# Moving weight roundings, stack loads, the last maxima and three loads of attended values in a two-layer attention and spectral kernel

## The chip, the cores and the metric

The kernel runs on one core of one Trainium2 chip. The time is the device time of one execution in microseconds (us); lower is better. Several runs are given for each kernel, and one further execution was recorded by the hardware profiler, which yields the trace that the rows below come from. The engines are PE (matmul), DVE (VectorE), ACT (ScalarE), POOL (GpSimd) and SP, which here only issues DMAs.

## The reference

Two layers are applied twice in turn to x, 2048 tokens of 576 features, all in float32:

```python
def _A_ref(x, wqkv, wo):               # called on layernorm(x)
    q, k, v = ...                      # x @ wqkv, 32 heads of 18
    scores = einsum("bhqd,bhkd->bhqk", q, k) * 18 ** -0.5
    # causal, sliding window of 256: 0 <= query - key < 256
    p = softmax(where(mask, scores, -1e9))
    return (p @ v) @ wo

def _B_ref(x, w_r, w_i):               # called on layernorm(x)
    return irfft2(rfft2(x) * (w_r + 1j * w_i), s=(S, D))

for _ in range(2):
    x = x + _A_ref(layernorm(x), A_wqkv, A_wo)
    x = x + _B_ref(layernorm(x), B_w_r, B_w_i)
```

## The kernel before

**Number format.** The products are float32 by splitting: a matrix is rounded to the type fp32r and the remainder is kept beside it, so that a product is a sum of three (high by high, high by low, low by high). For a weight block of the query and key projections the rounding `wqh` is a cast on ACT (L698) and the remainder `wql` a subtraction on POOL (L699; DVE for one block); `w_split(i)` issues both, and then `w_load(i + 2)`, a DMA on SP's queue (L896), into the buffer `wqr` that both have just read. That DMA therefore waits for the remainder.

**Stages of a layer A.** First the layernorm and the value projection. Then the query and key projections: nine blocks of 128 columns (i = 0 to 8), each for four chunks of 512 tokens (c = 0 to 3), fourteen matmuls each. A result `sg` (high and low, 512 KB) is sent to DRAM (`qk_d`, the send at L1145) and loaded back in another arrangement as stacks `qs` and `ks` of one group of four heads (`stack_load`, L1162). There are eight groups, and the stacks of two groups are held at a time. A stack of one group and one chunk comes in four pieces (two for q, two for k) of three DMAs of 72 KB.

**Rounds.** A round is one group of four heads and one tile of 128 tokens, 16 rounds a group, 128 in all. For round y the kernel first takes the row maxima of the scores (S on PE at L1187, the maximum on DVE at L1189), ten rounds ahead of the round x = y - 10 whose transposed scores E (L1219) go through the exponential on ACT (L1220) into a tile P, masked by selects on POOL (L1222, L1225). The maxima of four tiles (one chunk) are collected, transposed on PE (`tpm`), copied on ACT (`mt`, L1201) and written by two DMAs of 4 KB on SP's queue into one row of `qs` (L1203, `m_rows`), so that the score matmul itself subtracts them. E of round x reads tiles x, x+1 and x+2 of its group.

**The order of the work** is written out by hand. Ten opening rounds (t = -10 to -1) take maxima and seven matmuls of projections each. Then 59 mixed blocks p = 0 to 58 take two rounds each: for rounds 2p and 2p+1 eight S for ten rounds ahead and eight E, between them the matmuls of the projections, each in two halves on the two halves of the PE array (results `pj`, `pk`). Behind them stands what is called the value block here: the halves just ended are copied by ACT (L1129) and added by POOL (L1133, `total`), what is planned for the `end` of the block runs (send, divide and others), then U = P times v for rounds 2p-2 and 2p-1 (L1240), and in odd blocks `m_rows` of chunk (2p + 9) // 4. Work planned `early` stands ahead of the block's second score step and work planned `mid` in its middle. `loads(t)` issues the stack loads and `behind(t)` the work for the output projection. Twelve tail rounds follow (t = 118 to 129), which have no projections and no maxima, and then the output projection with the following layer B.

**Shared buffers.** The first projections' results `sg` of block i = 2 stand in buffers of the tag "P", six in number, which the tiles P take next: the exponentials of rounds 2 to 5 wait until these results have been sent.

**SP's queue** issues strictly in order, some 0.36 us for each DMA, and each DMA also waits for the one eight before it.

**The output projection** (class `Out`) is prepared in late rounds: `room` and `weights` load wo, `split` rounds it (cast on ACT at L751, remainder on POOL), `const` and `filters` load tables, `load_x` the residual, `attended(z, half)` loads results of three parts of the attention (512 KB each, L774) into `oraw`. Part 3 holds the last groups: its rows come through `store` (`op_d` from `o`, L1275), `pack` (L1282) and `attended(3, ...)` (L777); the very last group goes from `o7` straight into its place (L1278).

## Time and profile before

| | us |
|---|---|
| median of 3 runs | 1313.33 |
| lowest, highest | 1306.14, 1315.49 |
| the profiled execution | 1308.3 |
| its span | 1306.6 |
| PE busy in it | 1271.4 (97%) |
| first layer: mixed blocks, from 127.5 to | 423.3 |
| first layer: tail rounds, to | 445.3 |
| second layer: mixed blocks, from 796.3 to | 1091.4 |
| second layer: tail rounds, to | 1113.0 |

The mean granted clock of PE over the execution is 0.995. The starts of the value products U mark the blocks: the products of block p are the stretch of rows of L1240 with the same start in the timeline of PE. Rows of the timeline give start, duration, engine, line, operation, output and inputs, the number of instructions, and in brackets the idle time before them and what ended it.

### The profile page before, as it was taken

The page shows a single profiled execution, that of the slowest core. Times are in us where ns is not written, and L with a number is a line of the kernel's source. Part 1 is how long each engine was busy: PE and PEld are TensorE (multiplying, and loading weights), DVE is VectorE, ACT ScalarE, POOL GpSimd, SP SyncE. Part 2 cuts the span into 40 slices and gives each one's busy share as a digit, 9 for nine tenths or more (in the row PEclk, how much of TensorE's full clock was granted, in tenths as well). Part 3 has the DMA queues.
Part 4 walks back from the last instruction along what each step waited for, and adds up shares of the span by engine and source line. Part 5 has one row for each costly group of instructions (what it writes and reads, how often), then busy time and mean ns, then how long its engine had stood idle before and what let it go on. Part 6 is the DMA issues. An engine that isn't in the chain of part 4 may idle for free.

```text
span 1306.6 us, 35490 instructions
## 1 busy us (share of the span) xinstructions
PE 1271.4 (97%) x12115; PEld 1004.0 (77%) x12115; DVE 950.9 (73%) x3192; ACT 784.7 (60%) x1944; POOL 777.0 (59%) x1252
## 2 busy tenths in 40 slices
PE   9999999999999899999999999999999999899998
PEld 8986666666678699975989976666666676897587
DVE  5417799999999577766674148989999986575755
ACT  5532788888876544533355315788878868473233
POOL 2158788998877444567221196788878776113721
PEclk9999999999999999999999999999999999999999
DMA  6847666666666647688873368666666668497874
GB/s 204 222 150 210 211 210 222 229 205 195 206 218 204 181 135 229 199 272 252 281 253 77 88 209 221 201 221 199 206 196 191 201 206 258 134 348 257 278 256 163
DMA packets 179497, 274.37 MB, mean 210 GB/s; under 512 B 67743, under 2 KB 77727, under 8 KB 177989
## 3 DMA queue, kind: packets, MB, share of 16 engines
q1 hardware_dynamic: 167007, 243.63, 59.4%
q0 software_dynamic: 4656, 13.44, 4.0%
q10 hardware_dynamic: 7654, 15.03, 3.3%
q8 instruction: 97, 1.59, 0.5%
q14 instruction: 83, 0.68, 0.2%
HBM read 164.54 MB, written 114.81 MB: 214 GB/s over the span
## 4 chain that ended last, share of the span: by engine, by line
PE 79%; DMA 8%; ACT 4%; DVE 4%; POOL 2%; issue 2%; SPq 1%; DVEq 0%; ACTq 0%; POOLq 0%
PE pj L1115 11%; PE U L1240 11%; PE vps L1005 9%; PE S L1187 8%; PE pk L1115 7%; PE ops L802 7%; PE E L1219 5%; PE po L274 4%; PE pq L524 3%; PE p L503 2%; PE pf L274 2%; ACT P L1220 2%; PE pi L600 2%; DMA op_d<-o 2%; PE pz L312 2%
## 5 line engine op out<-in xcount | busy, mean ns | idle before, releaser
L1189 DVE CUSTOM_DVE_ANT_0 jk<-S,mask 128x384 bf16<-128x384 f32 (+2 forms) x1024 | 481.3, 527 | 31.1 <-PE S L1187 11.8
L1220 ACT ACTIVATE P<-E 128x384 f32<-128x384 f32 (+2 forms) x1024 | 411.7, 479 | 86.4 <-PE E L1219 41.9
L1219 PE MATMUL E<-qs,ks 64*128 64x384 f32 (+2 forms) x1024 | 320.8, 369 | 8.2 <-ACT P L1220 4.2
L1187 PE MATMUL S<-ks,qs 63*128 63x384 f32 (+2 forms) x1024 | 324.6, 370 | 1.1 <-issue 0.5
L1222 POOL TENSOR_SCALAR_AFFINE_SELECT P<-P 128x512 f32<-128x512 f32 x256 | 163.2, 637 | 119.5 <-ACT P L1220 114.1
L1219 PEld LDWEIGHTS E<-qs,ks 64*128 64x128 f32 x1024 | 179.9, 185 | 55.4 <-ACT P L1220 28.3
L1187 PEld LDWEIGHTS S<-ks,qs 63*128 63x128 f32 x1024 | 172.6, 185 | 61.3 <-DVE m L1189 36.7
L1240 PE MATMUL U<-P,vq 128*32 128x256 f32 (+2 forms) x3840 | 185.1, 329 | 0.8 <-POOL P L1222 0.8
L1240 PEld LDWEIGHTS U<-P,vq 128*32 128x32 f32 (+1 forms) x3840 | 107.1, 109 | 75.4 <-issue 11.1
L1115 PE MATMUL pj<-xh,wqh 64*128 64x512 f32 (+1 forms) x360 | 151.9, 422 | 0.0
L1225 POOL TENSOR_SCALAR_AFFINE_SELECT P<-P 128x512 f32<-128x512 f32 x224 | 141.9, 634 | 0.0
L1115 PE MATMUL pj<-xh,wql 64*128 64x512 f32 (+1 forms) x360 | 138.0, 423 | 0.0
L1115 PE MATMUL pj<-xl,wqh 64*128 64x512 f32 (+1 forms) x288 | 120.6, 419 | 0.0
L802 PE MATMUL ops<-oroom 128*128 128x290 f32 (+1 forms) x812 | 114.0, 297 | 1.6 <-DVE ofree L848 1.2
L802 PEld LDWEIGHTS ops<-oroom 128*128 128x128 f32 x812 | 110.4, 189 | 2.3 <-ACT ofree L836 1.4
L1115 PE MATMUL pk<-xh,wqh 64*128 64x512 f32 x230 | 92.6, 403 | 0.0
L1115 PE MATMUL pk<-xh,wql 64*128 64x512 f32 x230 | 90.1, 396 | 0.0
L1246 DVE STREAM_TRANSPOSE us<-U 128x256 f32<-128x256 f32 x128 | 56.7, 443 | 45.2 <-PE U L1240 43.0
L1189 DVE DVE_READ_ACCUMULATOR2_ANT m<- 128x1 f32 x1024 | 85.0, 83 | 0.0
L1115 PE MATMUL pk<-xl,wqh 64*128 64x512 f32 x184 | 73.6, 400 | 0.0
L789 POOL TENSOR_TENSOR oroom<-oraw,oroom 64x128 fp32r<-64x128 f32 x26 | 13.9, 535 | 99.3 <-ACT oroom L787 49.4
L1115 PEld LDWEIGHTS pj<-xh,wqh 64*128 64x128 f32 (+1 forms) x360 | 67.1, 186 | 7.2 <-issue 1.5
(521 smaller groups left out, 2870.5 us busy)
## 6 DMA issues: line engine op xcount, KB each, us to landing
qk_d<-sg SPq DMA_DIRECT2D x56, 512.0 KB
qs<-qk_d SPq DMA_DIRECT2D x384, 72.0 KB
ks<-qk_d SPq DMA_DIRECT2D x348, 72.0 KB
op_d<-o SPq DMA_DIRECT2D x56, 256.0 KB
v_d<-vt SPq DMA_DIRECT2D x32, 304.0 KB
vq<-v_d SPq DMA_DIRECT2D x16, 608.0 KB
wt<-in_w SPq DMA_DIRECT2D x16, 580.0 KB
ofree<-x SPq DMA_DIRECT2D x16, 580.0 KB
```

Source lines behind the costliest of these rows:

```text
L274: T.matmul(ps[:, c, 0:NF], tail[r] if si == 4 else hl_(si), dcs[b // 2][r, b % 2], start=mi == si == 0, stop=si == 4)
L802: self.nc.tensor.matmul(self.ps[u][n][:, 0:self.n], x, self.w[p][:, (2 * wk + n) * self.n:(2 * wk + n + 1) * self.n], start=first and i == ...
L1005: T.matmul(ps[:, n, 0:288], xT(xk, c), w[:, wk, n * 288:(n + 1) * 288], start=i == 0, stop=i == len(ks) - 1)
L1115: T.matmul(ps.rearrange("r (n p) -> r n p", n=NT) if second else ps, w[r, wk], x[r], start=s == 0, stop=s == len(ks) - 1)
L1187: T.matmul(ps[:, 0:N], q[b:b + 63, pair, i * 128:i * 128 + 128], k[b:b + 63, pair, lo:hi], start=True, stop=True)
L1189: V.tensor_tensor_reduce(out=jk[:, 0:N], in0=ps[:, 0:N], in1=mask[:, 384 - N:384], scale=1.0, scalar=-3e38, op0=ALU.add, op1=ALU.max, accu ...
L1219: T.matmul(ps[:, 0:nq], k[b:b + 64, pair, j * 128:j * 128 + 128], q[b:b + 64, pair, j * 128:j * 128 + nq], start=True, stop=True)
L1220: A.activation(p[:, hl_, 0:nq], ps[:, 0:nq], AF.Exp, scale=SC)
L1222: P.affine_select(out=p[:, :, 0:128], in_=p[:, :, 0:128], pattern=[[0, 4], [1, 128]], compare_op=ALU.is_ge, fill=0.0, base=0, channel_mult ...
L1225: P.affine_select(out=p[:, :, 256:384], in_=p[:, :, 256:384], pattern=[[0, 4], [-1, 128]], compare_op=ALU.is_gt, fill=0.0, base=0, channel ...
L1240: T.matmul(U[32 * h:32 * h + v.shape[1], (q0 - e) * 128:(q1 - e) * 128], v, pt[n, j][:, h, (q0 - j) * 128:(q1 - j) * 128], start=j == max( ...
L1246: V.transpose(us[n, c][:, 8 * k:8 * k + 8].rearrange("r b (a p) -> r (b a) p", a=2), U[:, 0:256].rearrange("r (p n) -> r n p", n=NT))
```

## The change

Seven edits, none of which changes what is computed:

1. In the mixed blocks `w_split` is no longer issued in the midst of the projection's matmuls (step 7 of chunk 2) but collected and issued behind the block's last projection, ahead of what is planned for its end. This concerns five weight blocks per layer.
2. Stack loads of groups 1 to 7 are issued 18 rounds ahead, one piece a round, all on SP. Before, group 1 came partly whole at t = -4 and partly 12 rounds ahead, group 2's first chunk at t = 6 to 12, the rest 20 rounds ahead, and a part of group 1 on POOL's queue.
3. The projections end one block later (48 for 47 in `ends`).
4. The roundings of wo stand at the end of blocks 53 to 57 instead of in mid round; their weights' loads come four rounds later.
5. `store` stands half a block earlier.
6. The last `m_rows` is issued ahead of `behind(117)`.
7. `attended(0..2, 0)` come in rounds 112 to 114 and `attended(0..2, 1)` in rounds 118 to 120, where all six stood in rounds 112 to 117.

```diff
-            ended = []
+            ended, splits = [], []
...
                     if opens and s == 7 and c == 2 and 0 < i < 8:
-                        w_split(i + 1)
+                        if half is None:
+                            w_split(i + 1)
+                        else:
+                            splits.append(i + 1)
...
-                            (P if which and (n == 0 and c > 1 or n == 1 and c == 0) else nc.sync).dma_start(
+                            (P if which and n == 0 and c > 1 else nc.sync).dma_start(
...
-                if t == -4:
-                    stack_load(1, 0)
-                n, c = divmod(t + (12 if t < 16 else 20), NT)
-                if 4 <= t < 16 or 1 < n < NQ and t >= 12:
-                    stack_load(1 if t < 16 else n, t // 4 if t < 16 else c // 4, (t % 4,))
-                if t in range(6, 14, 2):
-                    stack_load(2, 0, ((t - 6) // 2,))
+                n, c = divmod(t + 2, NT)
+                if 0 <= n < NQ - 1:
+                    stack_load(n + 1, c // 4, (c % 4,))
...
-                ends = [1 + 47 * u // 22 for u in range(23)]
+                ends = [1 + 48 * u // 22 for u in range(23)]
...
+                for k in range(5):
+                    plan(end, last - 6 + k, out.split, k)
...
                     ended.clear()
+                    while splits:
+                        w_split(splits.pop())
                     run(end, p)
...
-                            plan(mid, p + 3, store, n, c)
+                            plan(early, p + 3, store, n, c)
...
+                    if p == last - 1:
+                        m_rows(*divmod((2 * last + LEAD - 1) // 4, 4))
                     behind(2 * p + 1)
-                m_rows(*divmod((2 * last + LEAD - 1) // 4, 4))
...
-                if t == OB - 22:
+                if t == OB - 18:
                     out.room()
-                if t - OB + 22 in range(0, 10, 2):
-                    out.weights((t - OB + 22) // 2)
-                if t - OB + 16 in range(0, 10, 2):
-                    out.split((t - OB + 16) // 2)
+                if t - OB + 18 in range(0, 10, 2):
+                    out.weights((t - OB + 18) // 2)
...
-                if 0 <= t - (OB - 8) < 6:
-                    out.attended(*divmod(t - (OB - 8), 2))
+                if t - OB in (-8, -7, -6):
+                    out.attended(t - OB + 8, 0)
+                if t - OB in (-2, -1, 0):
+                    out.attended(t - OB + 2, 1)
```

Here OB is 120, `last` 59 and LEAD 10. The lines of the kernel after are numbered three higher from the middle on (the send is L1148, the stack loads L1165, the maxima L1206, U L1243).

**The opening of the first layer, queue of SP.** The rows follow the load of a group's values; `wqr` is a weight load, `qs` and `ks` from `qk_d` are stack pieces, `qk_d` from `sg` a send, and `qs` from `mt` the maxima (here those of the third chunk of the first group). Before:

```order
L896 DMA wqr_1458<-in_wqk 128x640
L1162 DMA qs_1059<-qk_d 18x2x512 x6
L1145 DMA qk_d<-sg_2_1467 128x2x512
L1145 DMA qk_d<-sg_3_1530 128x2x512
L1145 DMA qk_d<-sg_0_1588 128x2x512
L1203 DMA qs_1058<-mt_2_1764 2x4x128 x2
```

and after:

```order
L896 DMA wqr_1458<-in_wqk 128x640
L1148 DMA qk_d<-sg_2_1467 128x2x512
L1165 DMA qs_1059<-qk_d 18x2x512 x3
L1148 DMA qk_d<-sg_3_1518 128x2x512
L1165 DMA qs_1059<-qk_d 18x2x512 x3
L1165 DMA ks_1061<-qk_d 18x2x512 x3
L1148 DMA qk_d<-sg_0_1582 128x2x512
L1165 DMA ks_1061<-qk_d 18x2x512 x3
L1165 DMA qs_1059<-qk_d 18x2x512 x6
L1206 DMA qs_1058<-mt_2_1770 2x4x128 x2
```

The sends have moved ahead of the stack pieces, and the maxima behind eighteen of them where there were six.

**Block 11 of the first layer.** On POOL stand the selects of P, the remainder (L1142) and the sum (L1133) of projections' results, and the remainder of a weight block, `wql`. Before:

```order
L1142 TENSOR_TENSOR sg_1_2635<-sg_1_2635 128x512
L699 TENSOR_TENSOR wql_2788<-wqr_1458,wqh_2787 128x640
L1222 AFFINE_SELECT P_6_2779<-P_6_2779 128x4x128
L1225 AFFINE_SELECT P_6_2779<-P_6_2779 128x4x128
L1222 AFFINE_SELECT P_7_2828<-P_7_2828 128x4x128
L1225 AFFINE_SELECT P_7_2828<-P_7_2828 128x4x128
L1133 TENSOR_TENSOR sg_2_2857<-sg_2_2857 128x512
```

and after:

```order
L1145 TENSOR_TENSOR sg_1_2629<-sg_1_2629 128x512
L1225 AFFINE_SELECT P_6_2774<-P_6_2774 128x4x128
L1228 AFFINE_SELECT P_6_2774<-P_6_2774 128x4x128
L1225 AFFINE_SELECT P_7_2816<-P_7_2816 128x4x128
L1228 AFFINE_SELECT P_7_2816<-P_7_2816 128x4x128
L1136 TENSOR_TENSOR sg_2_2845<-sg_2_2845 128x512
L699 TENSOR_TENSOR wql_2854<-wqr_1458,wqh_2853 128x640
```

The remainder of the weights has moved behind four selects and the sum. On SP's queue at the same place stand the weight load that waits for that remainder, the store of a finished result (`op_d` from `o`), stack pieces, a send, and the maxima of the second group's last chunk. Before:

```order
L896 DMA wqr_2791<-in_wqk 128x640
L1275 DMA op_d<-o_3_2749 128x512
L1162 DMA ks_1060<-qk_d 18x2x512 x3
L1145 DMA qk_d<-sg_1_2635 128x2x512
L1203 DMA qs_1059<-mt_3_2889 2x4x128 x2
```

and after:

```order
L1278 DMA op_d<-o_3_2743 128x512
L1165 DMA qs_1058<-qk_d 18x2x512 x3
L896 DMA wqr_2857<-in_wqk 128x640
L1148 DMA qk_d<-sg_1_2629 128x2x512
L1206 DMA qs_1059<-mt_3_2883 2x4x128 x2
```

The weight load now stands directly ahead of the send and the maxima; it is the same at block 3 and in the second layer.

**The end of the mixed blocks, queue of SP,** from the last table of constants on (`mt7_3` are the last maxima, `o6_3` the last result of the seventh group; `dc` tables, `ofree` from `in_x` the residual, `oraw` attended values, `oroom` the filters). Before:

```order
L758 DMA dc4_7928<-dcr_62 128x580
L774 DMA oraw1_7825<-o_d_85 128x4x256
L766 DMA ofree_6992<-in_x 128x576
L774 DMA oraw0_7762<-o_d_85 128x4x256
L762 DMA oroom_6991<-gcr_63 128x512
L774 DMA oraw1_7825<-o_d_85 128x4x256
L1203 DMA qs1_1059<-mt7_3_8035 2x4x128 x2
L1275 DMA op_d_86<-o6_3_8011 128x512
```

and after:

```order
L758 DMA dc4_7911<-dcr_62 128x580
L766 DMA ofree_7184<-in_x 128x576
L1206 DMA qs1_1059<-mt7_3_8014 2x4x128 x2
L762 DMA oroom_7183<-gcr_63 128x512
L1278 DMA op_d_86<-o6_3_7992 128x512
L766 DMA ofree_7184<-in_x 128x576
L774 DMA oraw1_8047<-o_d_85 128x4x256 x2
L1285 DMA o_d_85<-op_d_86 16x2304
```

The last maxima and the last store of the seventh group now precede the filters or follow them directly, and the loads of attended values into `oraw1` stand behind them.

## The prediction

> **What bounds the kernel now.** I read the engine shares first, then the windows by stage, then, inside the attention stage, the starts of the value blocks in the timeline of TensorE.
>
> ```profile
> PE 1271.4 (97%) x12115; PEld 1004.0 (77%) x12115; DVE 950.9 (73%) x3192; ACT 784.7 (60%) x1944; POOL 777.0 (59%) x1252
> 145.40:423.30 277.90, 276.73 (x3458) 195.38 (x3454) 253.50 (x1004) 223.96 (x551) 231.46 (x324) 1.00 0.66 210
> 423.30:445.30 22.00, 18.31 (x268) 10.21 (x265) 11.89 (x26) 16.93 (x45) 12.68 (x21) 1.00 0.82 248
> ```
>
> After the window and its length the columns are busy microseconds of PE, weight loads, DVE, ACT and POOL, the granted clock, the DMA share and GB/s. PE is busy 97% of the span, and 276.7 of 277.9 us in the first layer's mixed blocks. There a stall of PE costs its full length, and work of ACT or POOL costs only what it delays PE. The layer's tail is different: PE is busy 18.3 of 22.0 us, so 3.7 us could go there.
>
> **The opening.** The edit that touches PE first is the one to the stack loads. Before, the SP queue reads: weight load, six pieces of a stack, send of a projection, maxima.
>
> ```profile
> 132.02 0.35 SPq L896 DMA_DIRECT2D wqr<-in_wqk  x1
> 132.42 2.17 SPq L1162 DMA_DIRECT2D qs<-qk_d  x6
> 134.69 2.16 SPq L1145 DMA_DIRECT2D qk_d<-sg  x3
> 137.29 1.87 SPq L1203 DMA_DIRECT2D qs<-mt  x2
> 139.65 1.71 ACT L1220 ACTIVATE P<-E 128x384 f32<-128x384 f32 x4 [2.39 <-DMA qk_d<-sg]
> 140.20 0.64 PE L1219 MATMUL E<-qs,ks 64*128 64x384 f32 x1 [2.08 <-ACT P L1220]
> 135.62 0.86 PE L1240 MATMUL U<-P,vq 128*32 128x256 f32 x16
> 143.99 1.51 PE L1240 MATMUL U<-P,vq 128*32 128x256 f32 x32
> 140.20:143.30 3.10, 3.10 (x16) 3.10 (x18) 1.60 (x6) 2.13 (x6) 1.22 (x2) 0.51 0.82 259
> 807.24 3.38 ACT L1220 ACTIVATE P<-E 128x384 f32<-128x384 f32 x8 [1.37 <-DMA qk_d<-sg]
> ```
>
> The exponentials write into buffers from which projections are still being sent, so ACT waits 2.39 us for the send, PE waits 2.08 us for ACT, and then PE runs 3.1 us at 0.51 of the clock. The block from 135.62 to 143.99 takes 8.37 us, where a later one takes 5.14 (308.19 to 313.33, quoted below): 3.2 us too much. The second layer has the same wait, 1.37 us on ACT; PE loses between 0 and that, and I take 0.9, above the middle since PE lost 2.08 of ACT's 2.39 above. Now the send stands right behind the weight load, ahead of the six pieces (2.17 us of issue), so it starts about 2.2 us sooner and both stalls go: **minus 4.1 us**.
>
> What is late next in that queue: the maxima of chunk 2 of the first group. They stood behind one weight load, six pieces and three sends; now they stand behind the weight load, three sends and eighteen pieces. A piece takes 2.17/6 = 0.36 us to issue, so twelve more make 4.3 us, less what the queue spent waiting on sends (2.16 us for three); issue moves from 137.3 to about 140 to 142. The group's first scores that need them come behind the value block of 143.99, whose products take some 1.4 us; without the 3.2 us that is 142.2. A maxima transfer takes between these two:
>
> ```profile
> 1058.57 3.63 DMA qs<-mt
> 124.67 7.29 DMA qs<-mt
> ```
>
> With the lower one it lands at 143.6 to 145.6, 1.4 to 3.4 us late if the first layer had no slack, and less in the second, where the queue is ahead. I take 2 us for both layers together: **plus 2.0** (bounds 0 and 7).
>
> **The roundings of the projections' weights.** Five blocks per layer had the cast on ACT and the remainder on POOL in their middle. I compare two such blocks with the blocks eight further on, which have the same place in the pattern and no rounding, by the starts of the value products:
>
> ```profile
> 183.89 0.86 PE L1240 MATMUL U<-P,vq 128*32 128x256 f32 x16
> 189.13 1.07 PE L1240 MATMUL U<-P,vq 128*32 128x256 f32 x20
> 194.27 1.07 PE L1240 MATMUL U<-P,vq 128*32 128x256 f32 x20
> 223.66 1.07 PE L1240 MATMUL U<-P,vq 128*32 128x256 f32 x20
> 228.42 0.84 PE L1240 MATMUL U<-P,vq 128*32 128x256 f32 x14
> 268.31 1.06 PE L1240 MATMUL U<-P,vq 128*32 128x256 f32 x18
> 273.80 1.07 PE L1240 MATMUL U<-P,vq 128*32 128x256 f32 x20
> 308.19 1.07 PE L1240 MATMUL U<-P,vq 128*32 128x256 f32 x20
> 313.33 1.05 PE L1240 MATMUL U<-P,vq 128*32 128x256 f32 x17
> 387.26 1.07 PE L1240 MATMUL U<-P,vq 128*32 128x256 f32 x20
> 392.71 1.07 PE L1240 MATMUL U<-P,vq 128*32 128x256 f32 x20
> L698 ACT CAST wqh<-wqr x18: 710/721/761, 56.1 to 983.0; 128x640 fp32r<-128x640 f32 x18
> L699 POOL TENSOR_TENSOR wql<-wqr,wqh x16: 1551/1559/1574, 56.9 to 984.3; 128x640 fp32r<-128x640 f32 x16
> 190.88 0.27 ACT L1201 ACTIVATE mt<-tpm 16x128 fp32r<-16x128 f32 x1 [0.32 <-PE tpm L1199]
> ```
>
> 5.24 against 4.76 us, and 5.49 against 5.14: the cast costs 0.48 and 0.35, some 0.4 each, ten times 4.0 us. In the value block it lands just where ACT waits 0.32 us for the transposed maxima (the last row), so of its 0.72 us up to 0.4 stay and delay the next exponentials; PE has value products to do there. I take 0.15 each (bounds 0 and 0.4): **minus 2.5**.
>
> **The roundings of wo** move likewise, in five blocks per layer. 387.26 to 392.71 is 5.45 us against 5.14: 0.31 each, and I count all of it, since these issue no transfer: **minus 3.1** (bounds 0 and 3.1).
>
> **The new wait.** The remainder on POOL is what the next weight load waits for (it overwrites what both roundings read). While that was mid block, nobody stood behind it. Now the queue of SP reads at the end of blocks 3 and 11 of each layer: weight load, send, maxima.
>
> ```profile
> 180.18 0.64 ACT L1129 COPY sg<-pk 128x512 f32<-128x512 f32 x1
> 181.10 1.29 POOL L1133 TENSOR_TENSOR sg<-sg 128x512 f32<-128x512 f32 x1
> 188.57 0.36 SPq L896 DMA_DIRECT2D wqr<-in_wqk  x1
> 191.17 1.63 SPq L1203 DMA_DIRECT2D qs<-mt  x2
> ```
>
> Before, the weight load goes out at 188.57, ahead of the value block of 189.13, and the maxima 2.04 us after the block's start. After, POOL first adds the halves just copied: the copy ends 1.5 us after the start of a block (two copies of 0.65 and a gap), the sum takes 1.29, the remainder 1.56, so the weight load goes out after some 4.3 us; behind it the weight load's own 0.36 and a send of like length, then the two maxima transfers (0.8 apart as in the row of 191.17): the second at about 5.7. With 3.63 us it lands 9.3 us after the block's start. The scores that need it are those of the block after next, which begin one block (5.14) and the value products (1.07 by the row of 194.27, and a score step and a projection step ahead, some 0.35) later: 6.6. That is a stall of 2.7 us; because a weight load and a 512 KB send go out just ahead of it I take 2.8: **four times 2.8 = plus 11.2** (bounds 0, if the transfer is as quick as 1 us, and 4.5). The other three roundings per layer end in blocks whose maxima are either absent (even blocks) or of a group's first chunk, which is read three blocks later.
>
> Does such a stall also slow the clock? Beside the opening's 0.51 after an idle of 2.08 us, the starts of the two output projections bear on it: the granted clock is the third number from the end of a window's row.
>
> ```profile
> 445.37 0.40 PE L802 MATMUL ops_pj<-oroom 128*128 128x288 f32 x1 [2.15 <-DVE us L1246]
> 445.40:448.40 3.00, 3.00 (x22) 3.00 (x23) 2.80 (x7) 0.00 (x0) 0.00 (x0) 1.00 0.66 169
> 1113.00 0.56 PE L802 MATMUL ops_pj<-oroom 128*128 128x290 f32 x1 [2.16 <-DVE us L1246]
> 1113.00:1116.20 3.20, 3.20 (x13) 3.20 (x14) 3.00 (x7) 0.00 (x0) 0.00 (x0) 0.51 0.61 159
> ```
>
> So of three idles of 2.08, 2.15 and 2.16 us the first and the last were followed by 3.1 us at half speed (1.5 us lost). I take two of the four new stalls: **plus 3.0** (bounds 0 and 6). [...]
>
> **The tail.** Before, the last maxima are issued behind the filters and the loads of attended values, which now come later.
>
> ```profile
> 432.39 0.44 PE L1219 MATMUL E<-qs,ks 64*128 64x384 f32 x2 [1.06 <-DMA qs<-mt]
> 440.94 0.72 DVE L787 CAST oroom<-oraw 128x512 fp32r<-128x512 f32 x1 [1.31 <-DMA o_d<-op_d]
> 1100.02 0.44 PE L1219 MATMUL E<-qs,ks 64*128 64x384 f32 x2 [0.80 <-DMA qs<-mt]
> ```
>
> The waits of 1.06 and 0.80 us for the maxima go; the packed last group lands sooner, since three loads of 512 KB stand behind it instead of before it, and the 1.31 us in which DVE waited for it shrinks, in both layers. That is 1.9 plus up to 2.6; with the 1.5 us of half clock at 1113 likely gone it is 0.5 to 6. I take **minus 4.0**. The three loads delayed are needed only in the output projection; if they came late there, up to 1.5 us of this would be given back. Spreading the projections over one more block removes only idle-filling matmuls; I count nothing, and the half block by which a finished result is stored earlier is covered, since its pack comes two blocks later.
>
> **The sum**: -4.1 + 2.0 - 2.5 - 3.1 + 11.2 + 3.0 - 4.0 = +2.5 on the profiled execution's 1308.3 us, so 1311. That execution lies 5 us under the median of the runs shown (1313.3), inside their spread of 0.7%; a measurement of this kernel can tell about 1%, 13 us, from no change.
>
> **The rivals.**
> 1. *The maxima are not late* (0.22). If the remainder slips in ahead of the sum's wait, or these transfers of 4 KB land in 1 to 2 us, the four stalls and the clock term fall away: 1311 - 14.2 = 1297; with nothing lost at the opening either 1295. For it: before, none of these maxima, issued 2 us into the block, made PE wait, so they land in under 4.6 us, and how far under no row tells. Against it: the 3.63 and 7.29 us.
> 2. *The weight load blocks the queue for longer* (0.13, slower). The one mechanism is the wait at blocks 3 and 11: if the maxima land as the slower row does (7.29 instead of 3.63), each stall is 6.3 us instead of 2.8, and every one is long enough for half clock: +14 + 3 = 1328. It decides from about 5 us per stall. For it: the load and the send just ahead on the same engines. [...]
> 3. *Little moves* (0.13). The casts cost the same in the value block, and the maxima land in 2.5 us: -4.1 - 3.1/2 - 4.0/2 + 4 x 1.5 = -1.7, so 1306.6. It differs little in time from the forecast and is told from it in the trace.
>
> **How the numbers follow.** The forecast case has 0.52, about 1303 to 1320 by its bounds. Rival 1 ends at 1295 to 1298, rival 2 at 1324 to 1330. A range of 1296 to 1323 leaves out rival 2 and half of rival 1's lower edge, nearly 2 in 10. Against the runs shown, faster by over 1% means under 1300: rival 1 nearly whole, 0.21. Slower by over 1% means over 1326: most of rival 2, 0.10. The rest, 0.69, is no change.
>
> **What the profile after would show.** Right: the block from 135.62 falls from 8.4 to near 5 us with no wait for a send; the blocks with roundings fall to their counterparts; the value blocks of 3 and 11 are followed, one block later, by PE waiting 2 to 4 us for the maxima, with the weight load in the SP queue some 4 us into the block; the tail has no wait for maxima. Wrong: no such wait (then rival 1), the casts moved showing up as waits of PE for ACT right behind the value block (then less gain), or a loss in the output projection for the attended values.

## The result and the profile after

| | us |
|---|---|
| before, median of 4 runs | 1311.95 (1306.14 to 1315.49) |
| after, median of 4 runs | 1325.12 (1324.33 to 1327.96) |
| ratio, with its 95% interval | 1.0109 (1.0068 to 1.015) |
| profiled execution and span after | 1324.91 and 1323.0 |

The kernel became 1.1% slower; the forecast was 1311, and the time lies 2 us above the upper end of the range. Between the two profiled executions the difference is 16.6 us. By the page of after PE is busy for 1273.9 us, about as long as before (1271.4).

The list of waits of PE says what was added (engine, line, what it waited for, microseconds in all, times, the longest). First before, then after:

```profile
PE ops_pj L802 <- DVE us L1246: 4.3, 2, 2.2
PE E L1219 <- ACT P L1220: 4.2, 7, 2.1
PE E L1219 <- DMA qs<-mt: 2.4, 4, 1.1
```

```profile
PE E L1222 <- DMA qs<-mt: 14.1, 8, 2.7
PE ops_pj L802 <- DVE us L1249: 10.2, 2, 5.1
PE E L1222 <- ACT P L1223: 1.5, 8, 0.3
```

The wait for ACT behind the sends is nearly gone, as was forecast. In its place stand 14.1 us for maxima, and at the start of the two output projections 10.2 us where it was 4.3.

**The opening after.** Timeline of SP's queue and of PE, first layer; then two rows of the second layer and one of the chain of waits, and two windows (length, busy PE and the other engines, granted clock third from the end):

```profile
138.18 2.97 SPq L1165 DMA_DIRECT2D qs<-qk_d  x6
141.26 1.25 SPq L1206 DMA_DIRECT2D qs<-mt  x2
136.07 0.86 PE L1243 MATMUL U<-P,vq 128*32 128x256 f32 x16
140.71 1.51 PE L1243 MATMUL U<-P,vq 128*32 128x256 f32 x32
144.60 0.41 PE L1222 MATMUL E<-qs,ks 64*128 64x384 f32 x1 [2.13 <-DMA qs<-mt]
148.91 1.82 PE L1243 MATMUL U<-P,vq 128*32 128x256 f32 x32
818.84 0.29 PE L1190 MATMUL S<-ks,qs 63*128 63x128 f32 x1 [1.25 <-DMA ks<-qk_d]
821.57 0.41 PE L1222 MATMUL E<-qs,ks 64*128 64x384 f32 x1 [2.44 <-DMA qs<-mt]
141.26 3.20 DMA qs<-mt
144.60:147.90 3.30, 3.30 (x25) 3.13 (x27) 1.68 (x10) 2.41 (x6) 1.13 (x2) 0.74 0.80 246
821.57:825.00 3.43, 3.43 (x22) 3.29 (x24) 1.57 (x9) 2.11 (x5) 1.06 (x2) 0.57 1.01 236
```

The block that took 8.37 us takes 4.64 (136.07 to 140.71). The next one takes 8.20 instead of 5.24: the maxima are issued at 141.26, behind the stack pieces, and land 3.2 us later. In the second layer that block takes 10.01 instead of 5.24, since PE waits there for two things in turn: 1.25 us for a stack piece of the second group, whose first maxima are taken in this block, and 2.44 us for the maxima of chunk 2. Both stalls for the maxima were followed by a slower clock (0.74 and 0.57).

**The value blocks with a rounding.** The queue at the end of block 3 and what it did two blocks on, then the maxima and the stall of block 11, the two stalls of the second layer, and the time that the maxima took:

```profile
153.19 0.36 SPq L896 DMA_DIRECT2D wqr<-in_wqk  x1
154.13 1.49 SPq L1206 DMA_DIRECT2D qs<-mt  x2
158.01 0.41 PE L1222 MATMUL E<-qs,ks 64*128 64x384 f32 x1 [1.78 <-DMA qs<-mt]
196.30 1.47 SPq L1206 DMA_DIRECT2D qs<-mt  x2
199.78 0.41 PE L1222 MATMUL E<-qs,ks 64*128 64x384 f32 x1 [2.01 <-DMA qs<-mt]
835.83 0.66 PE L1222 MATMUL E<-qs,ks 64*128 64x384 f32 x1 [2.72 <-DMA qs<-mt]
878.86 0.41 PE L1222 MATMUL E<-qs,ks 64*128 64x384 f32 x1 [1.82 <-DMA qs<-mt]
154.13 3.75 DMA qs<-mt
196.30 3.34 DMA qs<-mt
```

The weight load goes out 4.28 us after the value products of 148.91 began, the maxima 5.2 us after. What follows the stalls, by windows, as above:

```profile
158.00:161.00 3.00, 2.99 (x27) 2.49 (x29) 2.26 (x9) 2.52 (x6) 0.78 (x2) 1.00 0.65 177
199.70:203.00 3.30, 3.22 (x19) 2.93 (x21) 2.17 (x9) 2.06 (x5) 1.41 (x3) 0.67 0.61 173
835.80:839.20 3.40, 3.37 (x18) 3.17 (x20) 1.57 (x5) 1.76 (x4) 0.59 (x1) 0.51 0.61 196
878.80:882.10 3.30, 3.24 (x20) 2.85 (x21) 2.34 (x9) 2.14 (x6) 1.64 (x3) 0.69 0.62 169
```

Three of the four stalls were followed by a slower clock (0.67, 0.51 and 0.69).

**The tail,** first before, then after (first layer; the last two rows are the output projections of both layers):

```profile
423.35 1.51 PE L1240 MATMUL U<-P,vq 128*32 128x256 f32 x32
432.98 0.55 SPq L1282 DMA_DIRECT2D o_d<-op_d  x1
435.61 1.22 SPq L777 DMA_DIRECT2D oraw<-o_d  x2
```

```profile
428.71 1.51 PE L1243 MATMUL U<-P,vq 128*32 128x256 f32 x32
433.32 1.33 SPq L774 DMA_DIRECT2D oraw<-o_d  x2
435.58 0.58 SPq L1285 DMA_DIRECT2D o_d<-op_d  x1
436.26 3.71 SPq L1281 DMA_DIRECT2D ofree<-o  x4
440.52 0.60 SPq L774 DMA_DIRECT2D oraw<-o_d  x1
441.91 1.22 SPq L777 DMA_DIRECT2D oraw<-o_d  x2
448.25 0.43 DVE L787 CAST oroom<-oraw 128x512 fp32r<-128x512 f32 x1 [4.52 <-DMA oraw<-o_d]
452.06 0.61 PE L802 MATMUL ops_pj<-oroom 128*128 128x288 f32 x1 [5.11 <-DVE us L1249]
1130.13 0.61 PE L802 MATMUL ops_pj<-oroom 128*128 128x290 f32 x1 [5.09 <-DVE us L1249]
```

No score waits for the last maxima any more, but from the last value block to the output projection it takes 23.35 us (428.71 to 452.06) where it took 22.02, and 23.34 in the second layer where it took 21.51. Two of the moved loads (433.32) stand just ahead of the first pack (L1285), and between it and the load of the last attended part (L777) stand the four stores of the last group and the third moved load. That load goes out 13.2 us after the last value block, where it took 12.3 before, although the pack goes out 2.8 us sooner after it; DVE's first cast of the output projection starts 19.5 us after the value block instead of 17.6. The output projections begin at a granted clock of 0.50 in both layers (452.06 to 456.50 and 1130.13 to 1135.00), where before only the second did; what stands behind the tails differs by less than 1 us a layer.

The table adds up the difference by the starts of the value products in both traces. For the roundings it takes the rest of each layer's mixed blocks; block 3 had a rounding of its own, some 0.5 us a layer, which lies in its own row.

| us, both layers | forecast | measured |
|---|---|---|
| sends ahead of the pieces (block 2) | -4.1 | -5.0 |
| maxima of chunk 2 (block 3) | +2.0 | +7.7 |
| weight load ahead of the maxima (blocks 5, 13), with the clock | +14.2 | +12.9 |
| roundings in the value blocks | -5.6 | -4.9 |
| tail to the output projection | -4.0 | +3.2 |
| blocks 23 and 25 of the first layer | 0 | +2.3 |
| the rest | 0 | +0.3 |
| sum | +2.5 | +16.4 |

### The profile page after: what moved, and what is told of

Read it like the earlier page. It is cut to its first block, busy times and chain, and to the rows that moved or that the text cites. A ratio compares the mean times of both kernels' runs of the same rounds, so it can differ in the third digit from the quotient of the medians.

```text
span 1323.0 us, 35368 instructions
## 1 busy us (share of the span) xinstructions
PE 1273.9 (96%) x12059; PEld 1009.3 (76%) x12059; DVE 949.3 (72%) x3192; ACT 786.9 (59%) x1944; POOL 772.2 (58%) x1240
## 4 chain that ended last, share of the span: by engine, by line
PE 82%; DMA 8%; DVE 3%; ACT 2%; issue 2%; SPq 1%; POOL 0%; DVEq 0%; ACTq 0%; POOLq 0%
PE pj L1118 12%; PE U L1243 11%; PE S L1190 9%; PE vps L1005 9%; PE pk L1118 8%; PE ops L802 7%; PE E L1222 6%; PE po L274 4%; PE pq L524 3%; PE p L503 2%; DMA qs<-mt 2%; PE pi L600 2%; PE pf L274 2%; DMA yd<-ye 1%; PE pz L312 1%
## 5 line engine op out<-in xcount | busy, mean ns | idle before, releaser
L1222 PE MATMUL E<-qs,ks 64*128 64x384 f32 (+2 forms) x1024 | 320.2, 370 | 16.3 <-DMA qs<-mt 14.1
L1243 PE MATMUL U<-P,vq 128*32 128x256 f32 (+2 forms) x3840 | 185.5, 330 | 0.0
L1243 PEld LDWEIGHTS U<-P,vq 128*32 128x32 f32 (+1 forms) x3840 | 107.1, 109 | 75.4 <-issue 13.8
L1118 PE MATMUL pj<-xh,wql 64*128 64x512 f32 (+1 forms) x360 | 141.4, 432 | 0.0
L1118 PE MATMUL pk<-xh,wql 64*128 64x512 f32 x230 | 93.3, 408 | 0.0
L789 POOL TENSOR_TENSOR oroom<-oraw,oroom 64x128 fp32r<-64x128 f32 x26 | 13.9, 537 | 102.3 <-ACT oroom L787 52.5
```

Source lines behind the costliest of these rows:

```text
L1118: T.matmul(ps.rearrange("r (n p) -> r n p", n=NT) if second else ps, w[r, wk], x[r], start=s == 0, stop=s == len(ks) - 1)
L1222: T.matmul(ps[:, 0:nq], k[b:b + 64, pair, j * 128:j * 128 + 128], q[b:b + 64, pair, j * 128:j * 128 + nq], start=True, stop=True)
L1243: T.matmul(U[32 * h:32 * h + v.shape[1], (q0 - e) * 128:(q1 - e) * 128], v, pt[n, j][:, h, (q0 - j) * 128:(q1 - j) * 128], start=j == max( ...
```

## The experiments

A block is named here as in the code; the expectations below count one higher (their blocks 24 and 26 are 23 and 25 here) where they speak of blocks that waited early in the first layer, and as here for 5 and 13. All ratios are to the kernel before, on the same chip.

**1. The weight load behind the maxima.** The rounding stays where it is.

```diff
-                w_load(i + 2)
+                late_loads.append(i + 2)
+                if not hold_loads:
+                    w_load(late_loads.pop())
...
                     while splits:
+                        hold_loads.append(1)
                         w_split(splits.pop())
+                        hold_loads.pop()
...
                     if p % 2:
                         m_rows(*divmod((2 * p + LEAD - 1) // 4, 4))
...
+                    while late_loads:
+                        w_load(late_loads.pop())
```

> The kernel after, but in the value blocks the next weight load is issued behind the block's maxima instead of ahead of them; the roundings stay where the change put them. Theory (the weight load, which waits for the remainder on POOL, holds the SP queue): the four waits for maxima in blocks 5 and 13 of both layers (idle of PE 1.78, 2.01, 2.72 and 1.82 us, blocks of 6.99, 8.43, 9.32 and 8.13 us) go, each block comes to 4.9 to 5.2 us, and the time falls by 12.9 us to about 1312. Rival (the roundings themselves, on ACT and POOL, make the maxima late): the four blocks keep over 6.5 us each and the time stays within 3 us of 1325.

1310.96 us, ratio 1.0006 (0.9987 to 1.0024), 14 us less than after. The four blocks take 4.92, 4.92, 4.93 and 4.92 us. The timeline of SP in block 11 and PE's waits:

```profile
189.62 0.39 SPq L1151 DMA_DIRECT2D qk_d<-sg  x1
190.17 2.14 SPq L1209 DMA_DIRECT2D qs<-mt  x2
192.55 0.36 SPq L897 DMA_DIRECT2D wqr<-in_wqk  x1
PE E L1225 <- DMA qs<-mt: 3.2, 3, 2.0
```

With casts and remainders in the same place, only the order of two DMAs in the queue was changed, and 10.9 of the 14.1 us of waits for maxima went, 8.3 of them in the four blocks; the others were in the opening and in block 25, which differ from trace to trace. The theory holds. The tail is untouched, as it should be: PE's wait at the output projections is 10.3 us.

**2. The stack loads of before,** in the kernel after; the k pieces of group 1's first chunk are on POOL's queue again too.

```diff
-                n, c = divmod(t + 2, NT)
-                if 0 <= n < NQ - 1:
-                    stack_load(n + 1, c // 4, (c % 4,))
+                if t == -4:
+                    stack_load(1, 0)
+                n, c = divmod(t + (12 if t < 16 else 20), NT)
...
```

> The kernel after with the stack loads of before. Theory (in the opening the one wait was exchanged for a dearer one): the block with the wait for a send comes back (4.64 to about 8.4 us in the first layer, 4.63 to 5.9 in the second), the wait for the maxima of chunk 2 one block later goes (8.20 to about 5.0, and 10.01 to about 5.2), so minus 3.0 net, about 1322. Rival (the maxima of chunk 2 are late because of the three sends ahead of them, not of the eighteen stack loads): both waits stand in the trace and the time is about 1330.

1321.61, ratio 1.0087 (1.0061 to 1.0113). The block with the send takes 9.09 and 6.04 us again, the one behind it 5.73 and 4.76 instead of 8.20 and 10.01. So the chunk's maxima are late because of the loads, and the rival is out. These four blocks take 25.6 us in all, against 27.5 after. How much dearer the new wait is cannot be read from one pair: in the eight traces here with the stack loads of after (after, 1, 3 to 7 and 12) the sum lies between 23.2 and 27.5 us, seven of them above 25.8, and in the three with those of before (before, 2 and 10) between 24.6 and 25.6. In each of the eight PE also waits in block 3 of at least one layer, 0.6 to 2.0 us, for a stack piece of the second group.

**3 to 6. The end of the mixed blocks, by parts.** In the kernel after: the loads of attended values as before (3); all three parts as before (4); only the store as before (5); store and loads as before, the last maxima first (6). Edit 3 is the first hunk, 5 the second, 6 both, and 4 all three:

```diff
-                if t - OB in (-8, -7, -6):
-                    out.attended(t - OB + 8, 0)
-                if t - OB in (-2, -1, 0):
-                    out.attended(t - OB + 2, 1)
+                if 0 <= t - (OB - 8) < 6:
+                    out.attended(*divmod(t - (OB - 8), 2))
...
-                            plan(early, p + 3, store, n, c)
+                            plan(mid, p + 3, store, n, c)
...
-                    if p == last - 1:
-                        m_rows(*divmod((2 * last + LEAD - 1) // 4, 4))
                     behind(2 * p + 1)
+                m_rows(*divmod((2 * last + LEAD - 1) // 4, 4))
```

> The kernel after with the six loads of attended values interleaved in rounds 112 to 117 as before; the last maxima still go first and the store is still half a block earlier. Theory (the three loads put into the tail rounds hold up the packs and the loads of the last attended part behind them): from the value block of the last mixed block to the output projection it takes about 21 instead of 23.3 us in both layers and the clock stays full there, minus 6 us, about 1319. Rival (the earlier store, which swaps the first pack with the store of the last group, is what made the tail longer): 23 us stay, 1325.

> The kernel after with the whole end of the mixed blocks as before: loads of attended values, last maxima behind the filters, store in mid block. Theory: the tails are those of before, 22.0 and 21.5 us, with the waits of about 1 us for the last maxima, minus 4.7 us with the clock, about 1320, and about 1.5 us slower than with the loads alone moved back. Rival (the last maxima first are worth nothing): the same time as with the loads alone moved back, within 0.5 us in each tail of the trace.

> The kernel after with the store of a finished result in mid block again; everything else as after. Theory (the store half a block earlier swaps, on SP's queue, the first pack of the seventh group with the four stores of the last group, 3.7 us of issue, which then stand between that pack and the load of the last attended part): with the old order these stores are issued while the pack waits for its data anyway, the load goes out about 1 us earlier and the two tails fall from 23.3 to about 22.3 us, minus 2 us in all. Rival (what lengthens the tail is that the last maxima go first): 23.3 us stay.

> The kernel after with the loads of attended values and the store as before: of the changes at the end only the last maxima first is left. It stands between the version with the whole end as before (tails of 22.4 and 22.1 us) and the one with the loads alone moved back (24.6 and 24.8). Theory (the earlier store costs, the maxima gain nothing): tails of 22 to 22.5 us. Rival (the last maxima first cost 2 us): tails over 24 us.

| store | attended loads | last maxima | us, ratio | tail, first and second layer |
|---|---|---|---|---|
| early | late | first | 1325.12, 1.0109 (1.0068 to 1.015) | 23.35, 23.34 |
| early | before | first | 1327.29, 1.013 (1.0102 to 1.0159) | 24.57, 24.84 |
| mid | late | first | 1325.9, 1.0125 (1.0086 to 1.0163) | 22.46, 22.51 |
| mid | before | first | 1323.19, 1.0096 (1.0067 to 1.0124) | 21.95, 22.00 |
| mid | before | last | 1324.23, 1.0124 (1.009 to 1.0157) | 22.43, 22.10 |

The times do not separate these, and the tails in the traces do so only in part. Other traces here hold the same code of the tail: that of after stands in 1, 2 and 12, with tails of 23.49 and 23.27, 22.74 and 22.34, 23.41 and 24.93 us, and that of before in 10 and 11, with 22.02 and 23.61, 22.29 and 21.30. The same code differs by up to 2.6 us in one tail, so a smaller difference can come from the trace alone. My first theory, that the moved loads lengthen the tail, is refuted in the form expected: with the early store, moving them back shortens nothing (1.2 to 1.5 us longer in these traces). The early store costs 2.6 to 2.8 us with the loads of before, just beyond that spread and in both layers at once. With the late loads it costs 0.8 to 0.9, which is well within it; there the load of the last attended part goes out 13.3 and 13.5 us after the last value block with the store in mid block, no sooner than the 13.2 and 12.8 of after. The late loads cost 0.5 with the store in mid block, within the spread too.

The last maxima first show 0.5 and 0.1, which is nothing clear of the spread, and the waits say why: with the maxima last PE stood idle for 2.00 us in the tail of the first layer and 2.15 at the output projection, with the maxima first for 3.72 at the output projection alone. In the second layer 1.20 and 2.72 became 0.51 and 3.18. What was saved at the maxima was waited for at the last attended part.

**7. The load of the last attended part directly behind the first pack** (on the kernel of 1).

```diff
+                if t == OB:
+                    out.attended(3, 0)
...
-                if t - OB in (1, 2):
-                    out.attended(3, t - OB - 1)
+                if t == OB + 2:
+                    out.attended(3, 1)
...
-                    lag = {..., store: 4 if a in pending else 1, ...}[f]
+                    lag = {..., store: (7 if a[0] == NQ - 1 else 4) if a in pending else 1, ...}[f]
```

> The kernel with the weight load behind the maxima, and in the tail the load of the last attended part directly behind the first pack, with the last group's four stores two steps later. Theory (PE waits 5 us at the start of the output projection because that load stands behind four stores, 3.7 us, and another load): it goes out about 3.5 us earlier, the wait of PE falls from 5.1 to under 2 us in both layers, and with the clock full afterwards the time falls by 7 to 9 us against the version without it (1311), to about 1303. Rival (the packs and loads take as long as their bytes need, whatever the order): the wait stays over 4 us and the time at 1311.

1311.72, ratio 1.0017 (0.9997 to 1.0038): nothing gained of the 7 to 9 us expected, tails of 24.88 and 23.70. Two reasons stand in the timeline:

```profile
428.30 1.31 SPq L774 DMA_DIRECT2D oraw<-o_d  x2
430.76 0.58 SPq L1288 DMA_DIRECT2D o_d<-op_d  x1
436.98 1.21 SPq L777 DMA_DIRECT2D oraw<-o_d  x2
446.13 0.71 DVE L1276 STREAM_TRANSPOSE o<-us 128x512 f32<-128x512 f32 x1 [2.76 <-DMA ofree<-o]
448.57 0.61 PE L802 MATMUL ops_pj<-oroom 128*128 128x288 f32 x1 [6.65 <-DVE us L1252]
```

The load waits 6.2 us from the issue of the pack, which has two of the moved 512 KB loads just ahead of it, so it goes out 13.3 us after the last value block, no sooner than the 13.2 of after with the stores in between (12.7 and 12.8 in the second layer); and DVE then waits 2.76 us for the store that I had put later, since its buffer is needed again.

**8. Room in the opening** (on 7). The k pieces of group 1's first chunk go to POOL's queue as before the change, its other chunks two rounds later.

```diff
-                n, c = divmod(t + 2, NT)
-                if 0 <= n < NQ - 1:
+                n, c = divmod(t + (0 if 2 <= t < 16 else 2), NT)
+                if 0 <= n < NQ - 1 and not 2 <= t < 4:
                     stack_load(n + 1, c // 4, (c % 4,))
+                if t in (14, 15):
+                    stack_load(2, 0, (t - 14,))
```

> The same, and the stack loads of the second group thinned out in the opening: the k pieces of its first chunk on POOL's queue as before the change, its other chunks two rounds later, so that three sends and six pieces stand ahead of the maxima of chunk 2 where there were three sends and eighteen pieces. Theory (the eighteen pieces made these maxima late): the block after them falls from 8.1 and 8.5 us to about 5 in both layers, minus 6.5 us, about 1297. Rival (the sends make them late): these blocks keep over 7 us and the time stays.

1306.57, ratio 0.9979 (0.9959 to 1.0). The two blocks take 5.04 and 4.75 us where they took 8.20 and 10.01 after, and 9.76 and 7.39 in the kernel that this one was built on. The pieces ahead of the maxima made them late, not the sends, and the wait for a stack piece is gone with them. Block 2 of the first layer gives 1.2 us back (5.82 for 4.64). The time fell by 5.2 us against the kernel of 7, where 6.5 were expected; the 1297 of the expectation counted on the gain of 7, which had not come.

**9. The second half of the attended values last** (on 1 and 8, store in mid block).

```diff
-                if t - OB in (-2, -1, 0):
-                    out.attended(t - OB + 2, 1)
-                if t - OB in (1, 2):
-                    out.attended(3, t - OB - 1)
+                if t == OB:
+                    out.attended(3, 0)
+                if t - OB in (2, 3, 4, 5):
+                    out.attended(t - OB - 2, 1)
```

> Weight load behind the maxima, stack loads thinned out in the opening, the last maxima first, the store in mid block as before, and the three loads of the second half of the attended values behind the load of the last part's first half, which itself stands directly behind the first pack. Theory (the pack of the seventh group lands late because 512 KB loads stand just ahead of it in the DMA engines: 6.2 us from issue in the version with the load behind the first pack, 2.5 us before): the pack lands within 3 us, the first cast of DVE in the output projection starts about 16 us after the last value block instead of 18 to 19.5, PE waits 1 to 3 instead of 5 us, tails of 20 to 21 us, and the time is about 1300, below before. Rival (the packs and the load need their 7 us in any order): tails of 22 us or more, about 1303.

1306.2, ratio 0.996 (0.9941 to 0.998).

```profile
430.07 0.55 SPq L1288 DMA_DIRECT2D o_d<-op_d  x1
432.63 1.25 SPq L777 DMA_DIRECT2D oraw<-o_d  x2
437.65 0.87 DVE L787 CAST oroom<-oraw 128x512 fp32r<-128x512 f32 x1 [1.15 <-DMA o_d<-op_d]
442.24 0.61 PE L802 MATMUL ops_pj<-oroom 128*128 128x288 f32 x1 [2.15 <-DVE us L1252]
456.77 0.61 PE L802 MATMUL ops_pj<-oroom 128*128 128x288 f32 x1 [4.10 <-ACT oroom L796]
```

Without the large loads ahead, the load behind the pack goes out after 2.6 us instead of 6.2, DVE starts 16.2 us after the value block of 421.49 and both tails take 20.75 us: the theory holds there. But 14.5 us later PE waits 4.10 us for the last group's rows on ACT, and 3.43 at the same place in the second layer, so both layers give the gain back further on: the time is close to that of 8, not the 1300 expected.

**10. The roundings alone,** on the kernel before, weight load behind the maxima as in 1.

```diff
-                        w_split(i + 1)
+                        if half is None:
+                            w_split(i + 1)
+                        else:
+                            splits.append(i + 1)
...
+                for k in range(5):
+                    plan(end, last - 6 + k, out.split, k)
...
-                if t - OB + 16 in range(0, 10, 2):
-                    out.split((t - OB + 16) // 2)
```

> The kernel before with only the two moves of roundings into the value blocks, the next weight load issued behind the maxima; opening, stack loads, end and tail as before. Theory (the casts in mid block cost 0.4 us in ten blocks, those of wo 0.3 us in ten): the ten blocks with weights and the ten with wo come to those without, minus 6 us, about 1304, ratio 0.995. Rival (what the casts no longer cost mid block they cost in the value block): within 1.5 us of before.

1306.0, ratio 0.9963 (0.9944 to 0.9981). The timeline of PE, for the blocks that took 5.24 and 5.45 us:

```profile
182.45 1.51 PE L1246 MATMUL U<-P,vq 128*32 128x256 f32 x32
187.19 1.51 PE L1246 MATMUL U<-P,vq 128*32 128x256 f32 x32
384.42 1.51 PE L1246 MATMUL U<-P,vq 128*32 128x256 f32 x32
389.51 0.75 PE L1246 MATMUL U<-P,vq 128*32 128x256 f32 x12
```

4.74 and 5.09: the whole of what the casts cost in mid block is gone. So this part of the change is worth 4.9 us by itself (6 expected); the rival is out.

**11. The roundings and the first chunk of group 1** in single pieces from t = -2; all other stack loads and the tail as before.

```diff
-                if t == -4:
-                    stack_load(1, 0)
+                if -2 <= t < 2:
+                    stack_load(1, 0, (t + 2,))
```

> The kernel before with the two moves of roundings (weight load behind the maxima) and, of the stack loads, only the first chunk of the second group moved to one piece a round from t = -2 on; all other stack loads stand as before, 12 and 20 rounds ahead. Theory (the gain of the opening is that the sends go ahead of the pieces, and it keeps only as long as few pieces stand ahead of the maxima; the waits of 1 us and more around blocks 24 and 26 of the first layer come from the loads 18 rounds ahead): the two opening blocks take 10 to 10.7 us together in each layer where the version with the roundings alone has 11.5 and 13.0, blocks 24 and 26 of the first layer stay at 5.1 and 4.9, and the time is about 1303. Rival (the waits in the opening only move): no faster than 1306.

1303.53, ratio 0.9943 (0.9924 to 0.9963): the lowest median, 0.6% below before, though its interval overlaps those of 8 to 10. The two opening blocks take 10.15 and 10.29 us together, where 10 had 11.54 and 13.03. Blocks 23 and 25 of the first layer take 5.09 and 4.94.

**12. The projections' end as before,** on the kernel of 1.

```diff
-                ends = [1 + 48 * u // 22 for u in range(23)]
+                ends = [1 + 47 * u // 22 for u in range(23)]
```

> The kernel with the weight load behind the maxima, and the projections ending one block earlier again, as before the change. Theory (blocks 24 and 26 of the first layer, 6.11 and 6.18 us after the change against 5.08 and 4.93 before, are long because the later spread of the projections puts a send and its wait just ahead of the maxima there; with the stack loads of before they stayed long, 5.56 and 6.51): both come to 5.1 and 4.9, minus 1 to 2 us against the version without it. Rival (the stack loads 18 rounds ahead do it by their place): both stay above 5.4 us together with 11 us or more.

1309.85, ratio 1.0009 (0.9987 to 1.0031). Block 23 takes 5.08 instead of 5.94, block 25 5.81 instead of 5.31. With the old end and the old loads both are short (11), with either alone one or both stay long (2 and this). But the kernel of 7, with the new end and the new loads, has both short too (5.00 and 4.93), and that of 5 takes 8.15 and 4.87. Single traces do not tell what makes these blocks long, and it was not settled.

## Why the prediction was wrong

**What bounds the kernel** was read rightly: PE's own work hardly changed, and the time moved by its waits and the clock behind them.

**The sends in the opening** and **the roundings** came near the forecast (-5.0 for -4.1, -4.9 for -5.6). The 0.15 us a block that I charged for casts in the value block was not there: experiment 10 shows blocks as short as those without a rounding.

**The new wait** was right in its place and its cause, and nearly in its size: +12.9 for +14.2. The weight load went out at 4.28 us (4.3 forecast), and experiment 1 shows the cause. That the size came so near is in part luck, since two errors offset each other: the four idles were 1.78 to 2.72 us instead of 2.8, 8.3 in all for 11.2, and what came with them, the slow clock behind three of the four where two were forecast, was 4.6 for 3.0. The clock fell here after idles of 1.82 and 2.01 us (0.69 and 0.67 in the windows behind them) and stayed at 1.00 after 1.78.

**The maxima of chunk 2: a mis-sized term.** I took 2.0 with bounds 0 and 7; it was 7.7. The issue time was right (141.26, forecast 140 to 142), and a landing of 3.2 us too. But I counted a single stall of about 2 us for two layers, gave the second layer slack that it did not have (2.44 us of wait there, 2.13 in the first), and left out here the slow clock that I had charged for the other stalls (0.74 and 0.57 behind these two). And I did not ask when the stack pieces themselves would land: 1.25 us of the second layer's stall were a wait for one of them. Two stalls at the middle of my own bounds for one, 2.4, each with 1.5 for the clock, would have been 7.8, and that this meets 7.7 without the wait for the piece is chance; the eight traces with these loads put the term between 3.4 and 7.7.

**The tail: the step that failed.** Forecast -4.0, measured +3.2, and in all four traces with this tail (after, 1, 2 and 12) the two tails together are longer than before. The sum rested on the packed last group landing sooner, "since three loads of 512 KB stand behind it instead of before it". The first two of them stood ahead of its pack, and the load that depends on the pack went out later, 13.2 and 12.8 us after the last value block where before it took 12.3 and 11.9; DVE's wait of 1.3 us, which was to shrink, grew to 4.5, and the half clock at the start of the second output projection, which I had counted as likely gone, now stood at both (0.50). Experiments 7 and 9 show what those two loads go with: the dependent load goes out 6.2 and 6.0 us after the pack with them just ahead, 2.6 in both layers without, and 4.1 and 4.3 in experiment 5, where the four stores stand between those loads and the pack; how the two loads make it later was not shown. In the kernel after, the four stores between the pack and the load are not shown to delay it: with them moved behind it (7) or ahead of the pack (5) it goes out no sooner. I had also dismissed the earlier store with "its pack comes two blocks later"; in the tail it has no such distance, it changed places with the first pack in the queue, and with the loads of before that costs up to 2.8 us a layer (3 against 6). How the 3.2 us divide between loads and store stays open. Lastly I took each wait away by itself: the 1.06 and 0.80 us for the maxima went, but PE only arrived earlier at the wait behind them (4 and 6).

**Of the rivals,** the slower one came nearest in time (1328), by another mechanism than the one named: the four stalls with their clock were a little smaller than forecast, not larger. Of the 13.9 us between the sums, 7.2 come from the tail, 5.7 from the opening's maxima and 2.3 from blocks 23 and 25, which I had not foreseen and did not explain; the other rows take 1.3 back.

## What to carry to other kernels

Here a DMA that waited for POOL went out 4.28 us after the value products began, and the maxima behind it in SP's queue at 5.2 us; with it behind them (1), 10.9 of 14.1 us of PE's waits for maxima went, and the time fell by 14 us. So when work is moved, see whether its load should go behind what is urgent as well. Nor was a wait that was removed worth its length here: in the first layer idles of PE of 2.00 us in the tail and 2.15 at the output projection became one of 3.72 at the output projection (4 and 6). So follow the chain to its end, in the queue's new order, before you add waits up. In an order written by hand, an edit to the steady blocks must be read again where the steady state ends.

## What the runs showed of the hardware

The granted clock was lower for some 3 us after idles of PE as short as 1.82 us (0.69, 0.67 and 0.51 in three windows of 3.3 to 3.4 us) and stayed at 1.00 after 1.78 us in another; I had not expected it to fall after less than 2 us. After 2.13 and 2.44 us in the opening it was 0.74 and 0.57 over 3.3 and 3.4 us. Transfers of 4 KB took 3.20, 3.34 and 3.75 us from issue to landing in the trace of after, close to the 3.63 of before, whether the DMAs ahead were one weight load and a send or eighteen pieces; the 7.29 of before did not come again in these three. A load that depends on a pack of 144 KB went out 6.2 and 6.0 us after it with two loads of 512 KB just ahead (7), and 2.6 us after it without (9).
